# Batch 0 of a fused linear attention and SwiGLU kernel: both halves of q loaded in fp32 by one queue, q turned by products onto a bank of ones, order redone

## The chip, the cores and the metric

The kernel runs on one core of one Trainium2 chip. The metric is the device time of one execution in microseconds. Seven executions of the kernel before took 314.73 us in the median (314.56 to 316.13).

A core has five engines with an instruction stream each: TensorE (PE, products into PSUM; PEld is its loading of weights), VectorE (DVE), ScalarE (ACT, which computes exp, ln and silu), GpSimd (POOL) and SyncE (SP). In this kernel POOL and SP issue the transfers: POOL those that also convert fp32 to fp16 on the way, SP those that do not convert. Each engine works through its own stream in program order and waits on semaphores.

## The reference

Inputs q, k, v have the shape (8 batches, 8 heads, 576 positions, 64). With phi(x) = x + 1 for x > 0 and exp(x) otherwise:

```
kv  = einsum('bhsd,bhse->bhde', phi(k), v)
z   = sum over s of phi(k)
num = einsum('bhsd,bhde->bhse', phi(q), kv)
den = einsum('bhsd,bhd->bhs', phi(q), z) + 1e-06
x   = (num / den), heads side by side: 4608 tokens x 512
out = ((silu(x @ w_gate) * (x @ w_val)) @ w_out)      # 512 -> 1536 -> 512
```

The feed-forward part has nearly all of the products: 4608 x 512 x 1536 twice and 4608 x 1536 x 512 once.

## The kernel before

**Tiling.** Nine groups (g = 0 to 8) of 512 tokens each go through the feed-forward part. A group takes eight units of 64 tokens; a batch has nine units (J = 9), so group 0 is made of the first eight units of batch 0. The main loop (L626) runs over groups: twelve blocks of 128 columns of w_gate and w_val (`l1`, L287; products L291), each followed by silu and multiplication (`l1_post`, L280), then four output tiles (`l2_mm`, L297; products L298). The attention of later batches is slipped in between.

**The head.** Group 0 can only start when batch 0's attention has given x^T. Lines 331 to 481 do that in an order written out by hand (`manual_schedule`); each engine follows the order of the lines. The eight heads are worked on as two halves of four, called lp 0 and lp 1: lp picks the half in every transfer and tile.

The steps of batch 0, with the names used later:

- Transfers. SP loads q's lp 0 into `q32` and k's lp 0 into `k32`, both in fp32 (L332). POOL loads q's lp 1 (L334), k's lp 1, v, and the weights, all to fp16 (L102, L111).
- `warm(n, w)` (L121) issues n products of ones that nothing reads; `WARM` holds their counts. They keep TensorE active.
- q: the fp32 half is cast to fp16 `qr` by VectorE (L431) and ScalarE (L432). `qtr` (L365) transposes q on TensorE into fp16 PSUM. phi is then applied to the transposed q, three steps for 1024 columns (`t_phi`, L380): exp by ScalarE into `qT`, min(exp, 1) by VectorE (L382), and max(q, 0) added by VectorE (L383). For lp 1 the last step is split into two halves of 512 (`t_add_half`, L420).
- k: exp by ScalarE (`ek`, L436 and `exp_k`), max(k, 0) by VectorE (`kp`, L437 and `mx_k`), min(exp, 1) by VectorE (`mn_k`, L144). The two parts are never added: products take `kp` and then `ek` into the same accumulator.
- z: `zt` (L392) sums the positions by products with a matrix of ones; `zr_copy` (L397) copies the sum to `Zr`.
- kv: `kv_corner` (L178, products L184) takes 72 small products per lp; `r_copy` (L194) copies them to `R`.
- den and num: `t_corners` (L416, products L253) multiplies qT by Zr or R. `lnrd` (L401) makes 1/den by ScalarE as exp(-ln(den)), two ln and two exp steps per lp.
- x: `x_t` (L412) multiplies num by 1/den on VectorE (L410) into xT, four tiles of 128 x 512 over lp and half.
- The first two blocks of group 0 are run by `l1_mm` (L272, products L275) chunk by chunk of xT, so that they can start before all of xT is there.

The PSUM pairs are named `pp4`; X and Y are pairs made of halves of two of them. The order of the lines also fixes what stands in each engine's stream behind a wait.

Of the kernel before, what the change touches and what calls it, by code (L numbers as in the profile page):

```python
# [7 lines left out]
FP32 = mybir.dt.float32  # L8
FP16 = mybir.dt.float16
# [4 lines left out]
P = 128  # L14
# [3 lines left out]
def kernel(  # L18
# [21 lines left out]
    EPS = 1e-6  # L40
    SC = 4096.0
    NB = 3
    WARM = (32, 8, 8, 6, 3, 3)

    sb = ctx.enter_context(tc.tile_pool(name="sb", bufs=1))
    pp = ctx.enter_context(tc.tile_pool(name="ps", bufs=1, space=bass.MemoryType.PSUM))
# [15 lines left out]
    Zr = many([P, 2, 2, D], FP16, "Zr")  # L62
    rd = many([P, 2, 512], FP16, "rd")

    q32 = sb.tile([P, 2, J * D], FP32, name="q32")
# [19 lines left out]
    idx = sb.tile([P, P], mybir.dt.int32, name="idx")  # L85
    gate = sb.tile([P, 1], FP16, name="gate")
    epsb = sb.tile([P, 1], FP32, name="epsb")

    pp4 = [[pp.tile([P, 512], FP32, name=f"pp_{2 * i + e}") for e in range(2)] for i in range(4)]
    ring = list(pp4)  # L90
# [27 lines left out]
    def act(out, in_, func=AF.Copy, scale=1.0, bias=0.0):  # L118
        nc.scalar.activation(out=out, in_=in_, func=func, bias=bias, scale=scale)  # L119
# [9 lines left out]
    def jl(t, b, lp):  # L129
        return t[b % 2][:, lp, :, :].rearrange("p j (l d) -> p l j d", d=D)  # L130
# [4 lines left out]
    def exp_k(b, lp):  # L135
        act(jl(ek, b, lp), lj(kr, b, lp), AF.Exp)
# [248 lines left out]
    def t_phi_main(b, lp, ps):  # L385
        return t_phi(qT[b][:, lp, 0:8, :, :].rearrange("p j h c -> p (j h c)"), ps[:, :].bitcast(FP16))
# [30 lines left out]
        for (b, j0, j1, c0) in units(g)[1]:  # L417
            corners(ps, W[b], b, lp, j0, j1, c0)

    def t_add_half(lp, ps, h):  # L420
        a = qT[0][:, lp, 4 * h:4 * h + 4, :, :].rearrange("p j h c -> p (j h c)")
        nc.vector.scalar_tensor_tensor(out=a, in0=ps[:, 256 * h:256 * h + 256].bitcast(FP16), scalar=0.0, in1=a,  # L422
                                       op0=ALU.max, op1=ALU.add)

    k32v = k32[:, :, :].rearrange("p l (j d) -> p l j d", d=D)
    pq = pp4[0]
    kvp[0] = pp4[1]
    X = [pp4[0][0], pp4[3][0]]
    Y = [pp4[3][1], pp4[0][1]]
    ph = [t_phi_main(0, lp, pq[lp]) for lp in range(2)]  # L430
    nc.vector.tensor_copy(out=qr[0][:, 0, :], in_=q32[:, 0, :])  # L431
# [5 lines left out]
    nc.vector.tensor_scalar(out=jl(kp, 0, 0), in0=k32v, scalar1=0.0, scalar2=None, op0=ALU.max)  # L437
    warm(WARM[1])
    zt(0, 0, X[1], kp, True, False)
    ph[0][1]()  # L440
    ph[0][2]()
    warm(WARM[2], 2)
    qtr(0, 1, pq[1])
    ph[1][0]()
    exp_k(0, 1)
    mn_k(0, 0)
    warm(WARM[3], 2)
    zt(0, 0, X[1], ek, False, True)
    zr_copy(0, 0, X[1])
    mx_k(0, 1)  # L450
    warm(WARM[4], 2)
    t_corners(0, Zr, 0, pp4[2])
    lnrd(pp4[2], 0)
    ph[1][1]()
    zt(0, 1, Y[0], kp, True, False)
    t_add_half(1, pq[1], 0)
# [5 lines left out]
    t_add_half(1, pq[1], 1)  # L462
    zr_copy(0, 1, Y[0])
    t_corners(0, R, 0, X)
    t_corners(0, Zr, 1, Y)
    lnrd(Y, 1)
    x_t(0, 0, X, (0,))
    kv_corner(0, 1, kp, True, False)
    kv_corner(0, 1, ek, False, True)
    x_t(0, 0, X, (1,))  # L470
    r_copy(0, 1, 2, "VV")
    l1_mm(0, 0, pp4[2], (0,))
    l1_mm(0, 1, X, (0,))
    t_corners(0, R, 1, pp4[1])
    x_t(0, 1, pp4[1])
    for c in (1, 2, 3):
        l1_mm(0, 0, pp4[2], (c,))
# [259 lines left out]
```

## Time and profile before

| | |
|---|---|
| median of seven executions | 314.73 us (314.56 to 316.13) |
| profiled execution, its time | 316.34 us |
| profiled execution, its span | 314.6 us |
| TensorE busy | 307.1 us (98% of the span) |
| VectorE busy | 204.0 us (65%) |
| ScalarE busy | 151.4 us (48%) |
| mean granted TensorE clock | 0.995 |
| first product of the main loop (L291) | 20.14 us after the start of the span |

The span runs from the first to the last instruction; the execution's time has 1.74 us around it. The profile gives, for a stretch of the span, each engine's busy time, the granted clock of TensorE (1.00 is full) and what the transfers moved. The timeline lists instructions in order of time; in square brackets stands how long the engine had been idle before, and which event ended that. "issue" there means that the engine waited for nothing that the profile shows.

### The profile page before, as it was taken

The page shows a single profiled execution, that of the slowest core. Times are in us where ns is not written, and L with a number is a line of the kernel's source. Part 1 is how long each engine was busy: PE and PEld are TensorE (multiplying, and loading weights), DVE is VectorE, ACT ScalarE, POOL GpSimd, SP SyncE. Part 2 cuts the span into 40 slices and gives each one's busy share as a digit, 9 for nine tenths or more (in the row PEclk, how much of TensorE's full clock was granted, in tenths as well). Part 3 has the DMA queues.
Part 4 walks back from the last instruction along what each step waited for, and adds up shares of the span by engine and source line. Part 5 has one row for each costly group of instructions (what it writes and reads, how often), then busy time and mean ns, then how long its engine had stood idle before and what let it go on. Part 6 is the DMA issues. An engine that isn't in the chain of part 4 may idle for free.

```text
span 314.6 us, 5728 instructions
## 1 busy us (share of the span) xinstructions
PE 307.1 (98%) x2289; PEld 145.8 (46%) x2289; DVE 204.0 (65%) x357; ACT 151.4 (48%) x229; POOL 47.4 (15%) x72
## 2 busy tenths in 40 slices
PE   7899999999999999999999999999999999999994
PEld 6534444444544454445444544444444444444442
DVE  3744788899789666978598749874991434134420
ACT  5844839738653755356435743475331333133311
POOL 8655345300000230023000500000000000000000
PEclk9989999999999999999999999999999999999999
DMA  8999999994612396129703890314022400140014
GB/s 217 199 198 200 206 207 226 244 206 83 140 33 39 52 181 168 37 40 162 200 11 65 119 243 1 75 33 102 2 56 60 94 2 1 33 102 0 0 35 100
DMA packets 41163, 32.82 MB, mean 104 GB/s; under 512 B 16432, under 2 KB 36144, under 8 KB 41136
## 3 DMA queue, kind: packets, MB, share of 16 engines
q0 software_dynamic: 20464, 18.29, 37.0%
q1 hardware_dynamic: 20592, 14.13, 18.5%
q8 instruction: 18, 0.29, 0.3%
q14 instruction: 9, 0.07, 0.1%
q10 hardware_dynamic: 80, 0.03, 0.0%
HBM read 37.75 MB, written 9.44 MB: 150 GB/s over the span
## 4 chain that ended last, share of the span: by engine, by line
PE 95%; DMA 1%; DVE 1%; issue 0%; SPq 0%; ACT 0%
PE pp L291 57%; PE pp L298 30%; PE pp L275 3%; PE pp L253 2%; PE pp L184 2%; DMA k<-in_k_dram 1%; PE pp L123 1%; PE pp L369 1%; DVE qT L422 0%; DVE kp L437 0%; PE pp L211 0%; PE pp L394 0%; DVE osb L321 0%; DVE Zr L398 0%; SPq L332 0%
## 5 line engine op out<-in xcount | busy, mean ns | idle before, releaser
L119 ACT ACTIVATE sil<-pp 128x512 f16<-128x512 f32 x108 | 63.4, 597 | 103.5 <-PE pp L291 97.4
L291 PE MATMUL pp<-xT,wg 128*128 128x512 f16 x416 | 106.8, 379 | 0.0
L291 PE MATMUL pp<-xT,wv 128*128 128x512 f16 x416 | 106.8, 379 | 0.0
L284 DVE SCALAR_TENSOR_TENSOR hT<-pp,sil 128x512 f16<-128x512 f32 x108 | 72.3, 681 | 49.4 <-PE pp L291 35.7
L298 PE MATMUL pp<-wo,hT 128*128 128x512 f16 (+2 forms) x444 | 97.2, 374 | 0.6 <-DVE osb L321 0.6
L298 PEld LDWEIGHTS <-hT 128*128 128x128 f16 x444 | 41.8, 98 | 49.8 <-issue 2.1
L291 PEld LDWEIGHTS <-wv 128*128 128x128 f16 x416 | 40.7, 98 | 49.1
L291 PEld LDWEIGHTS <-wg 128*128 128x128 f16 x416 | 40.7, 98 | 48.4
L321 DVE TENSOR_SCALAR osb<-pp 128x512 f32<-128x512 f32 (+1 forms) x19 | 12.9, 682 | 30.7 <-PE pp L298 30.7
L119 ACT ACTIVATE osb<-pp 128x512 f32<-128x512 f32 (+1 forms) x18 | 10.3, 574 | 34.8 <-PE pp L298 34.8
L119 ACT ACT_TABLE_LOAD x13 | 16.7, 1283 | 2.3 <-PE pp L291 2.1
L119 ACT ACTIVATE ek<-kr 128x1152 f16<-128x1152 f16 x15 | 16.8, 1155 | 0.1
L228 DVE TENSOR_TENSOR qp<-qp,rden 128x1152 f16<-128x1152 f16 x12 | 16.2, 1347 | 0.0
L219 DVE TENSOR_REDUCE den<-prod 128x18 f32<-128x1152 f16 x12 | 16.1, 1344 | 0.0
L668 POOL COPY gate<-qT 128x1 f16<-128x1 f16 x4 | 1.0, 256 | 99.3 <-DMA qT<-qp 99.3
L119 ACT ACTIVATE eq<-qr 128x1152 f16<-128x1152 f16 x12 | 13.2, 1147 | 0.0
L270 DVE TENSOR_SCALAR xT<-pp 128x512 f16<-128x512 f32 (+1 forms) x14 | 8.8, 667 | 6.6 <-PE pp L253 6.6
L102 POOL DMA_DIRECT2D vr<-in_v_dram x16 | 11.6, 728 | 9.2 <-PE pp L291 3.4
L102 POOL DMA_DIRECT2D qr<-in_q_dram x15 | 10.9, 732 | 7.8 <-DMA vr<-in_v_dram 1.9
L102 POOL DMA_DIRECT2D kr<-in_k_dram x15 | 10.8, 720 | 7.5 <-DMA wo<-in_moe_w_out_dram 1.9
L146 DVE TENSOR_SCALAR ek<-ek 128x1152 f16<-128x1152 f16 x16 | 7.7, 479 | 6.5 <-ACT ek L119 6.5
L158 DVE TENSOR_TENSOR kp<-ek,kp 128x1152 f16<-128x1152 f16 x14 | 10.6, 758 | 0.5
(71 smaller groups left out, 186.6 us busy)
## 6 DMA issues: line engine op xcount, KB each, us to landing
out_dram<-osb SPq DMA_DIRECT2D x70, 128.0 KB, 3.3
vr<-in_v_dram POOLq DMA_DIRECT2D x16, 288.0 KB, 10.0
qr<-in_q_dram POOLq DMA_DIRECT2D x15, 288.0 KB, 11.4
kr<-in_k_dram POOLq DMA_DIRECT2D x15, 288.0 KB, 9.6
wo<-in_moe_w_out_dram POOLq DMA_DIRECT2D x3, 512.0 KB, 13.0
wg<-in_moe_w_gate_dram POOLq DMA_DIRECT2D x5, 256.0 KB, 9.5
wv<-in_moe_w_val_dram POOLq DMA_DIRECT2D x5, 256.0 KB, 9.0
q<-in_q_dram SPq DMA_DIRECT2D x1, 576.0 KB, 3.7
```

Of the source, the lines that this page charges most:

```text
L102: nc.gpsimd.dma_start(out=dst[b % NB][:, 2 * lp:2 * lp + 2, :], in_=src[b].rearrange("(l a) (c j) d -> (a c) l (j d)", a=2, j=J)[:, 2 * lp ...
L119: nc.scalar.activation(out=out, in_=in_, func=func, bias=bias, scale=scale)
L146: nc.vector.tensor_scalar(out=a, in0=a, scalar1=1.0, scalar2=None, op0=ALU.min)
L158: nc.vector.tensor_tensor(out=a, in0=ek[b % 2][:, lp, :, :], in1=a, op=ALU.add)
L219: nc.vector.tensor_reduce(out=den[:, c, :], in_=prod[:, :, :].rearrange("p j (l d) -> p (j l) d", d=D), axis=AX.X, op=ALU.add)
L228: nc.vector.tensor_tensor(out=qv, in0=qv, in1=rden[:, c, :].unsqueeze(2).to_broadcast([P, 2 * J, D]), op=ALU.mult)
L270: nc.vector.tensor_scalar(out=dst, in0=ps[l2][:, c0:], scalar1=1.0 / SC, scalar2=None, op0=ALU.mult)
L275: nc.tensor.matmul(out=ps[h][:, :], lhsT=w[:, c, P * fb:P * fb + P], rhs=xT[g % 2][:, c, :], start=(c == 0), stop=(c == 3))
L284: nc.vector.scalar_tensor_tensor(out=hT[g % 2][:, fb, :], in0=ps[1][:, :], scalar=SC, in1=s[:, :], op0=ALU.mult, op1=ALU.mult)
L291: nc.tensor.matmul(out=ps[h][:, :], lhsT=w[:, c, P * fb:P * fb + P], rhs=xT[g % 2][:, c, :], start=(c == 0), stop=(c == 3))
L298: nc.tensor.matmul(out=l2p[(g, t)][:, n0:n1], lhsT=hT[g % 2][:, fb, P * t:P * t + P], rhs=wo[:, fb, n0:n1], start=(fb == 0), stop=(fb == F ...
L321: nc.vector.tensor_scalar(out=o[:, n0:n1], in0=ps[:, n0:n1], scalar1=1.0 / SC, scalar2=None, op0=ALU.mult)
```

## The change

It touches batch 0's head alone.

- SP now loads q's lp 0, q's lp 1 and k's lp 0, in this order, all in fp32 (`q32` is twice as large). POOL's load of q's lp 1 goes.
- The lp 1 half of q is cast to fp16 by two casts on VectorE.
- q is no longer transposed into fp16 PSUM. `q_one` first fills two PSUM pairs with ones, by products of a matrix of 1/128 with ones (each 512 columns wide); `q_turn` adds the transposed q to that by products with the identity. PSUM then holds q + 1 in fp32.
- phi is exp(PSUM - 1), by ScalarE (`q_exp`), and min(max(PSUM, 1), exp), by VectorE (`q_phi`): one VectorE step in the place of two, in pieces of 512 columns.
- The numbers and widths of the fillers change, and one run of them is added ahead of the first feed-forward products.
- The order changes: both halves of q are turned and given exp before k's exp; the second half's q_phi comes after both k halves' steps; Zr's corners of lp 1 come before R's of lp 0; the second R's corners come between the first two products of `l1_mm` and the rest.

```diff
-    WARM = (32, 8, 8, 6, 3, 3)
+    WARM = (20, 14, 30, 4, 3, 3)
...
-    def warm(n, w=1, ps=None):
+    def warm(n, w=128, ps=None):
         for _ in range(n):
-            nc.tensor.matmul(out=(ps or pp4[2][1])[:, 256:256 + P * w], lhsT=ones[:, :],
-                             rhs=ones[:, :].unsqueeze(1).to_broadcast([P, w, P]), start=True, stop=True)
+            nc.tensor.matmul(out=(ps or pp4[1][1])[:, 256:256 + w], lhsT=ones[:, :],
+                             rhs=ones[:, 0:1].to_broadcast([P, w]), start=True, stop=True)
...
-    for (src, dst) in ((q, q32), (k, k32)):
-        nc.sync.dma_start(out=dst[:, :, :],
-                          in_=src[0].rearrange("(l a) (c j) d -> (a c) l (j d)", a=2, j=J)[:, 0:2, :])
-    ld(q, qr, 0, 1)
+    for (src, dst, h) in ((q, q32, 0), (q, q32, 2), (k, k32, 0)):
+        nc.sync.dma_start(out=dst[:, h:h + 2, :],
+                          in_=src[0].rearrange("(l a) (c j) d -> (a c) l (j d)", a=2, j=J)[:, h:h + 2, :])
...
+    nc.vector.memset(part[:, :], 1.0 / P)
...
+    nc.vector.memset(m1[:, :], -1.0)
...
+    def q_one(pair_):
+        for h in range(2):
+            nc.tensor.matmul(out=pair_[h][:, :], lhsT=part[:, :], rhs=ones[:, 0:1].to_broadcast([P, 512]),
+                             start=True, stop=False)
+
+    def q_turn(lp, pair_):
+        for l2 in range(2):
+            for j in range(J - 1):
+                nc.tensor.matmul(out=pair_[j // 4][D * l2:D * l2 + D, P * (j % 4):P * (j % 4) + P],
+                                 lhsT=qr[0][:, 2 * lp + l2, D * j:D * j + D], rhs=id16[:, :],
+                                 start=False, stop=(j % 4 == 3))
+
+    def q_half(lp, h):
+        return qT[0][:, lp, 4 * h:4 * h + 4, :, :].rearrange("p j h c -> p (j h c)")
+
+    def q_exp(lp, h, pair_):
+        act(q_half(lp, h), pair_[h][:, :], AF.Exp, bias=m1[:, 0:1])
+
+    def q_phi(lp, h, pair_):
+        a = q_half(lp, h)
+        nc.vector.scalar_tensor_tensor(out=a, in0=pair_[h][:, :], scalar=1.0, in1=a, op0=ALU.max, op1=ALU.min)
...
+    qa, qb = pp4[2], pp4[0]
     nc.vector.tensor_copy(out=qr[0][:, 0, :], in_=q32[:, 0, :])
     act(qr[0][:, 1, :], q32[:, 1, :])
+    nc.vector.tensor_copy(out=qr[0][:, 2, :], in_=q32[:, 2, :])
+    nc.vector.tensor_copy(out=qr[0][:, 3, :], in_=q32[:, 3, :])
     warm(WARM[0])
-    qtr(0, 0, pq[0])
-    ph[0][0]()
+    q_one(qa)
+    q_one(qb)
+    q_turn(0, qa)
+    q_exp(0, 0, qa)
+    q_exp(0, 1, qa)
+    warm(WARM[1], 64)
+    q_turn(1, qb)
+    q_exp(1, 0, qb)
+    q_exp(1, 1, qb)
+    warm(WARM[2], 64)
     act(jl(ek, 0, 0), k32v, AF.Exp)
+    exp_k(0, 1)
+    q_phi(0, 0, qa)
+    q_phi(0, 1, qa)
     nc.vector.tensor_scalar(out=jl(kp, 0, 0), in0=k32v, scalar1=0.0, scalar2=None, op0=ALU.max)
...
+    mn_k(0, 0)
     zt(0, 0, X[1], kp, True, False)
...
+    warm(WARM[3], 256)
     zt(0, 0, X[1], ek, False, True)
     zr_copy(0, 0, X[1])
...
+    warm(WARM[4], 256)
     t_corners(0, Zr, 0, pp4[2])
     lnrd(pp4[2], 0)
...
+    mx_k(0, 1)
     mn_k(0, 1)
+    q_phi(1, 0, qb)
+    q_phi(1, 1, qb)
     kv_corner(0, 0, kp, True, False)
     kv_corner(0, 0, ek, False, True)
+    zt(0, 1, Y[0], kp, True, False)
     zt(0, 1, Y[0], ek, False, True)
+    zr_copy(0, 1, Y[0])
     r_copy(0, 0, 1, "VV")
...
     t_corners(0, Zr, 1, Y)
     lnrd(Y, 1)
-    x_t(0, 0, X, (0,))
+    t_corners(0, R, 0, X)
+    x_t(0, 0, X)
     kv_corner(0, 1, kp, True, False)
     kv_corner(0, 1, ek, False, True)
-    x_t(0, 0, X, (1,))
     r_copy(0, 1, 2, "VV")
+    warm(WARM[5], 256, pp4[2][1])
     l1_mm(0, 0, pp4[2], (0,))
+    t_corners(0, R, 1, pp4[1])
     l1_mm(0, 1, X, (0,))
-    t_corners(0, R, 1, pp4[1])
     x_t(0, 1, pp4[1])
```

More of the change, by code (lines that the diff above doesn't have):

```diff
@@ L63 @@
     rd = many([P, 2, 512], FP16, "rd")
-    q32 = sb.tile([P, 2, J * D], FP32, name="q32")
+    q32 = sb.tile([P, HL, J * D], FP32, name="q32")
     k32 = sb.tile([P, 2, J * D], FP32, name="k32")
@@ L87 @@
     epsb = sb.tile([P, 1], FP32, name="epsb")
+    m1 = sb.tile([P, 1], FP32, name="m1")
+    part = sb.tile([P, P], FP16, name="part")
     pp4 = [[pp.tile([P, 512], FP32, name=f"pp_{2 * i + e}") for e in range(2)] for i in range(4)]
@@ L418, in t_corners @@
             corners(ps, W[b], b, lp, j0, j1, c0)
[L420 to L423, printed above, removed]
+    def q_one(pair_):
[15 more added lines that the diff above has]
+        nc.vector.scalar_tensor_tensor(out=a, in0=pair_[h][:, :], scalar=1.0, in1=a, op0=ALU.max, op1=ALU.min)
     k32v = k32[:, :, :].rearrange("p l (j d) -> p l j d", d=D)
-    pq = pp4[0]
     kvp[0] = pp4[1]
@@ L429 @@
     Y = [pp4[3][1], pp4[0][1]]
-    ph = [t_phi_main(0, lp, pq[lp]) for lp in range(2)]
+    qa, qb = pp4[2], pp4[0]
     nc.vector.tensor_copy(out=qr[0][:, 0, :], in_=q32[:, 0, :])
     act(qr[0][:, 1, :], q32[:, 1, :])
+    nc.vector.tensor_copy(out=qr[0][:, 2, :], in_=q32[:, 2, :])
+    nc.vector.tensor_copy(out=qr[0][:, 3, :], in_=q32[:, 3, :])
     warm(WARM[0])
-    qtr(0, 0, pq[0])
-    ph[0][0]()
+    q_one(qa)
[8 more added lines that the diff above has]
+    warm(WARM[2], 64)
     act(jl(ek, 0, 0), k32v, AF.Exp)
+    exp_k(0, 1)
+    q_phi(0, 0, qa)
+    q_phi(0, 1, qa)
     nc.vector.tensor_scalar(out=jl(kp, 0, 0), in0=k32v, scalar1=0.0, scalar2=None, op0=ALU.max)
-    warm(WARM[1])
+    mn_k(0, 0)
     zt(0, 0, X[1], kp, True, False)
[L440 to L447, printed above, removed]
+    warm(WARM[3], 256)
     zt(0, 0, X[1], ek, False, True)
     zr_copy(0, 0, X[1])
-    mx_k(0, 1)
-    warm(WARM[4], 2)
+    warm(WARM[4], 256)
     t_corners(0, Zr, 0, pp4[2])
     lnrd(pp4[2], 0)
-    ph[1][1]()
-    zt(0, 1, Y[0], kp, True, False)
-    t_add_half(1, pq[1], 0)
+    mx_k(0, 1)
     mn_k(0, 1)
+    q_phi(1, 0, qb)
+    q_phi(1, 1, qb)
     kv_corner(0, 0, kp, True, False)
     kv_corner(0, 0, ek, False, True)
+    zt(0, 1, Y[0], kp, True, False)
     zt(0, 1, Y[0], ek, False, True)
+    zr_copy(0, 1, Y[0])
     r_copy(0, 0, 1, "VV")
-    t_add_half(1, pq[1], 1)
-    zr_copy(0, 1, Y[0])
-    t_corners(0, R, 0, X)
     t_corners(0, Zr, 1, Y)
     lnrd(Y, 1)
-    x_t(0, 0, X, (0,))
+    t_corners(0, R, 0, X)
+    x_t(0, 0, X)
     kv_corner(0, 1, kp, True, False)
     kv_corner(0, 1, ek, False, True)
-    x_t(0, 0, X, (1,))
     r_copy(0, 1, 2, "VV")
+    warm(WARM[5], 256, pp4[2][1])
     l1_mm(0, 0, pp4[2], (0,))
+    t_corners(0, R, 1, pp4[1])
     l1_mm(0, 1, X, (0,))
-    t_corners(0, R, 1, pp4[1])
     x_t(0, 1, pp4[1])
```

## The prediction

> **What bounds the kernel now.** I read the page first (share of the span, slices, chain), then the first 21 us by windows of 1 us, then the timeline of that stretch. Times below are us from the start of the span.
>
> ```profile
> span 314.6 us, 5728 instructions
> ...
> PE   7899999999999999999999999999999999999994
> ...
> PE 95%; DMA 1%; DVE 1%; issue 0%; SPq 0%; ACT 0%
> ```
>
> TensorE carries the chain from about 20 us to the end, and nothing there is edited. So the change is worth exactly what it moves one event: the first product of L291, at 20.14. Ahead of it TensorE waits for others, and once its clock falls. Windows of 1 us (columns: busy time of PE, PEld, DVE, ACT, POOL, then the granted clock, DMA share, GB/s):
>
> ```profile
> 14.00:15.00 1.00, 0.86 (x59) 0.79 (x59) 0.00 (x0) 1.00 (x2) 0.60 (x1) 0.69 1.47 200
> 15.00:16.00 1.00, 1.00 (x4) 0.37 (x4) 0.36 (x2) 0.95 (x3) 1.00 (x3) 0.50 1.44 194
> 16.00:17.00 1.00, 1.00 (x6) 0.13 (x4) 0.00 (x0) 1.00 (x1) 0.72 (x2) 0.50 1.44 194
> 17.00:18.00 1.00, 1.00 (x7) 0.28 (x4) 0.50 (x1) 0.13 (x1) 0.63 (x1) 0.60 1.51 212
> 18.00:19.00 1.00, 1.00 (x6) 0.47 (x5) 0.79 (x2) 0.00 (x0) 0.74 (x1) 1.00 1.38 187
> ```
>
> The clock is halved from 14.38 to 17.80 (the shares 0.69 and 0.60 give the edges). The 3.41 us before that were thin:
>
> ```profile
> 10.97:14.38 3.41, 1.94 (x114) 1.29 (x104) 2.97 (x8) 3.25 (x6) 1.67 (x3) 1.00 1.43 193
> ```
>
> The timeline of the same stretch, cut to the events that the change moves (start, duration, engine, line):
>
> ```profile
> 4.48 0.46 DVE L431 CAST qr<-q 128x576 f16<-128x576 f32 x1 [1.15 <-DMA q<-in_q_dram]
> 5.91 0.76 DVE L437 TENSOR_SCALAR kp<-k 128x1152 f16<-128x1152 f32 x1 [0.98 <-DMA k<-in_k_dram]
> 6.80 1.15 ACT L119 ACTIVATE ek<-k 128x1152 f16<-128x1152 f32 x1
> 7.48 1.23 DVE L383 SCALAR_TENSOR_TENSOR qT<-pp,qT 128x1024 f16<-128x1024 f16 x1
> 8.62 0.45 DVE L146 TENSOR_SCALAR ek<-ek 128x1152 f16<-128x1152 f16 x1
> 9.60 0.29 DVE L398 TENSOR_SCALAR Zr<-pp 128x128 f16<-128x128 f32 x1 [0.52 <-PE pp L394]
> 10.60 0.68 ACT L119 ACTIVATE lnt<-pp,epsb 128x512 f32<-128x512 f32 x1
> 10.62 0.69 DVE L422 SCALAR_TENSOR_TENSOR qT<-pp,qT 128x512 f16<-128x512 f16 x1
> 14.14 0.38 PE L184 MATMUL pp<-vr,kp 64*64 64x64 f16 x22 [0.81 <-issue]
> 16.75 0.64 PE L253 MATMUL pp<-qT,R 64*64 64x512 f16 x4
> 17.50 1.29 DVE L410 SCALAR_TENSOR_TENSOR xT<-pp,rd 128x512 f16<-128x512 f32 x2 [2.13 <-PE pp L253]
> 20.14 1.03 PE L291 MATMUL pp<-xT,wg 128*128 128x512 f16 x4
> ```
>
> The reader is to see that VectorE (L437 to L410) is nearly unbroken from 5.9 to 13.9 while k's exp is done at 7.96 and waits for L383; and that at 14.14 TensorE stops for 0.81 in the middle of one group (after 14 of 36 products with the same inputs), put down to "issue". The instruction queue moved one block of 16 KB between 11.8 and 12.9, so I read the stop as a wait for instructions.
>
> **What the low clock cost.** At full clock L275 products follow each other by 0.216 (18.63, 18.85), at half by 0.42. Redone at full clock from 14.14: rest of the kv products to 14.62, four L275 to 15.49, corners of R at 15.49, x from 16.0 to 17.3, eight more products behind a 0.15 wait, L291 at 18.5. The drop cost 20.14 - 18.5 = 1.64. The profiled execution took 316.34; without the drop 314.70, which is the median shown (314.73, lowest 314.56). So I take the median execution as one with little or no drop, and the executions above 315 as ones that met it. The fair rival of the new head is 18.5.
>
> **The change, part by part.**
>
> SP's queue: one transfer more there, one fewer on POOL. q's first half lands as before (4.48), the second takes k's place (5.91), k is third. SP's issue (0.45) delays nobody: SP's next work is the output. POOL's first 0.83 issue goes, so idx and the masks come earlier, hidden, since id16 is first needed at 4.99. First k landed 1.43 after q, so third it lands at 7.34 if SP's data go ahead of POOL's, and at 8.77 if POOL's take every second packet. From 2 to 5 us, with POOL's transfers issued from 1.25 on, only SP's queue moved data:
>
> ```profile
> q1 hardware_dynamic: 469, 1.04, 95.9%
> ```
>
> I take 7.34. The Trainium skill (DMA: Bandwidth & Descriptors, Issuing engines are not separate DMA queues) says that transfers of all issuing engines interleave on the same 16 DMA engines and that another issuer saves only issue time; this speaks against the move and for 8.77, and the row above disagrees for this stretch. By the rule the sum below ends 0.1 later. POOL's data start 1.4 later with 1.4 less of q in them, so k's other half (8.9), v and the weights keep their times.
>
> First products: 20 fillers at 0.107 (32 took 3.41) and four 512-wide ones onto the ones bank (0.43 at half, 0.22 at full clock) end by 4.9 at the latest; q's cast, needed first, is ready at 4.94. Nothing. Two memsets (0.17, 0.06): hidden by the same wait.
>
> VectorE: out go two L382 (0.43), L383 (1.23), two L422 (0.69), 3.47; in come four steps like L422 and L410 (0.69, next start 0.61 later) and two casts (0.46, next start 0.38 later), 3.68. ScalarE: out two exps of 1024 (1.02), in four of 512 like lnt (0.68, next start 0.58 later): +0.4. So no engine is relieved; what counts is order.
>
> In order: q's first products as L369 (4.99), exps from 5.8 and 6.4. Casts of the second half 5.91 and 6.29, to 6.75. Fillers of 64 columns have no row; between 0.03 (half of L123's 0.056) and 0.056 each, I take the upper, since the same weights are loaded; 14 end by 6.6, 30 by 9.0, beside the waits. Second products end 7.4, exps 7.4 and 8.0, so ScalarE is free at 8.55. Only then k's exp: 8.55 to 9.7, against 7.96 before. VectorE: the two steps of q's first half 6.66 and 7.27, max of k 7.88 to 8.64, then it stands for k's exp, with max and min of the other k half and the second q steps queued behind. L146 at 9.75 (+1.13), Zr at 10.7, corners 11.05, ln/exp from 11.6 instead of 10.60; their eight steps (10.60 to 15.83 before) end at 16.8. VectorE from 10.7: 0.21, 0.37, 0.37 (Zr, max, min), two of 0.61, Zr 0.20, R 0.35: R at 13.4, against 11.95.
>
> Corners of R on TensorE at 13.45. Here the products before them number 223, the number before the stop at 14.14 of the old kernel, so the instruction wait should fall here. Bounds: nothing, or until 14.14 as before (+0.6). The block before it ends in the second filler run, at about 7.6, against about 8.0 in the old order, so I take 13.55, nearer the lower. Then x at 14.1 and 14.7 to 15.3, R copies to 15.65, corners of the second R at 15.7 (15.49 in the old kernel at full clock), and 14 instead of 12 products behind them: 14 x 0.216 + 0.22 = 3.24. x is ready in time (16.9, 17.6 for products at 17.2, 18.1). L291 at 18.95.
>
> **Sum.** 18.95 against 20.14: -1.19 on the profiled execution, 316.34 - 1.19 = 315.15; against the 314.73 of the median, +0.4. No drop of the clock is in it. By start-to-start spacing (36 kv products 0.30, a zt run 0.2, four corners 0.22, a wide filler 0.11) the window that lost the clock held about 1.1 us of products: 0.14 and 0.34 of kv, 0.2, two times 0.22. The thinnest 3.41 us of the new order, 10.2 to 13.6, holds 2.0: kv 0.6, zt 0.6, three fillers 0.33, corners 0.44. Nothing shows where between 1.1 and 2.0 the limit lies. The Trainium skill (TensorE: Matmul & The Clock Gate, What's actually happening) halves the clock after an idle window of about 3.4 us; the trace lost it after a window that was half busy. By the rule neither kernel would lose the clock and the sum would be the same 18.95 against 18.5.
>
> 0.3% (0.94 us) is about what a measurement of this kernel can tell from no change.
>
> **Rivals.**
> (a) Slower: the clock falls in the new kernel too. Between about 10 and 15.7 TensorE waits for Zr, R and x; if a window of that stretch counts as thin, the 3.41 us after it do half of their work: +1.7 where all of them are products, about +0.8 where half falls on waits, 315.95 to 316.85. It decides if more than half of the executions meet it. For it: the waits go on until 15.7, in the old kernel to 14.6. Against: the fillers and all kv products lie inside them.
> (b) Slower: the instruction block comes as late as before, at 14.14: corners of R wait 0.6 more, 315.75.
> (c) Faster: k's exp is not late, because the half-size exps overlap more than I charge (0.50 between the two sil), and the steadier clock also takes away the 0.17 to 1.6 that half of the executions now lose: 18.2, 314.4. It passes the bound where L291 starts 1.4 earlier than forecast, at 17.55 (313.75).
> (d) No effect: the head ends where it did, 314.7.
>
> **Chances.** Forecast (314.8 to 315.6, its own range) 0.47; (a) 0.18, of which 0.15 over the bound; (b) and other lateness past 315.7 0.12; (c) 0.15, of which 0.11 under 313.8; (d) 0.08. Slower 0.27, faster 0.11, same 0.62. The range leaves out the faster tail of (c) and the full price of (a): 314.2 to 316.4.
>
> **What would show it.** Right: q's second cast pair at 5.9; exp of k at 8.5 with VectorE idle before L146 until about 9.7; Zr near 10.7; R near 13.4; corners of the second R near 15.7 as the last wait of TensorE; clock 1.00 from 5 us on; L291 near 19.0. Wrong: a clock of 0.5 after 11 us, an "issue" stop beyond 13.6, k landing after 8.5, or L291 before 18.3.

## The result and the profile after

The changed kernel takes 318.47 us in the median of twelve executions, against 315.29 for the kernel before in 31 executions. The ratio is 1.0091, with a 95% interval of 1.0066 to 1.0116, so the change is slower by 0.9%. The forecast was 315.15 with a range of 314.2 to 316.4, and it is missed on the slow side, by 3.3 us.

The profile that came with the changed kernel is of an execution that no other resembles: 1822.38 us, all of it on TensorE, whose products of 512 columns took 1.7 us each while the profile gave a granted clock of 1.00. From its page:

```profile
span 1820.6 us, 5776 instructions
...
L293 PE MATMUL pp<-xT,wg 128*128 128x512 f16 x416 | 589.3, 1707 | 0.0
```

It tells nothing of the change, whose other eleven executions took 316.89 to 320.27. I therefore ran the changed kernel again, unedited, and read the result from that profile (318.80 us, clock 0.987; median of five 318.80, ratio 1.011, 1.0071 to 1.0149). It is the first of the experiments.

> The changed kernel itself, unedited, once more, since its first profile shows a TensorE at about a sixth of its rate throughout (512-wide products 1.7 us apart) and can't be laid beside the old one. Three theories for the 2.9 us that it lost. Clock: the granted clock is 0.5 in one or two stretches of 3.4 us before 21 us, and the first product of the main loop (L293) starts at 21 to 23, each stretch in product work costing up to 1.7. Instructions: an idle of TensorE put down to issue, over 0.8 us long, ahead of L293, at a clock of 1.00. Late k: the max of k (L469) starts after 9 because k lands late, and all that follows with it. If none shows and L293 starts near 19, the loss is in the main loop, and the shares of L293 and L300 there have grown.

The lines of its page that answer to those shown of the kernel before:

```profile
span 317.0 us, 5776 instructions
...
PE   8699999999999999999999999999999999999994
...
PE 91%; DVE 3%; DMA 3%; ACT 1%; SPq 0%; issue 0%; DVEq 0%
PE pp L293 56%; PE pp L300 27%; DMA k<-in_k_dram 3%; PE pp L277 2%; PE pp L255 2%; PE pp L186 2%; DVE qT L386 1%; ACT ek L121 1%; PE pp L125 0%; ACT L582 0%; DVE qT L385 0%; DVE ek L148 0%; PE pp L397 0%; SPq L334 0%; DVE kp L160 0%
```

The second digit of PE's slices is 6 where it was 8. The chain that ended last has 3% of the span on one transfer of k, which had 1% before. The chain of the first 26 us, in order of time (start, duration, what), says the same more sharply:

```profile
1.76 8.02 DMA k<-in_k_dram
9.78 0.02 issue
9.80 1.17 ACT ek L121
10.98 0.02 issue
11.00 0.72 DVE ek L148
```

From SP's third issue at 1.76 until 9.78 the kernel's end depends on nothing but k's way into the chip. The timeline has the events that the prediction named:

```profile
5.83 0.46 DVE L452 CAST qr<-q 128x576 f16<-128x576 f32 x1 [1.12 <-DMA q<-in_q_dram]
7.28 1.27 ACT L121 ACTIVATE qT<-pp,m 128x512 f16<-128x512 f32 x2 [0.29 <-PE pp L431]
9.80 1.16 ACT L121 ACTIVATE ek<-k 128x1152 f16<-128x1152 f32 x1 [1.26 <-DMA k<-in_k_dram]
10.62 0.39 PE L397 MATMUL pp<-ob,kp 128*128 128x2 f16 x9 [2.12 <-DVE kp L469]
12.20 0.29 DVE L401 TENSOR_SCALAR Zr<-pp 128x128 f16<-128x128 f32 x1 [0.49 <-PE pp L397]
18.82 0.41 PE L255 MATMUL pp<-qT,R 64*64 64x512 f16 x4
22.19 1.03 PE L293 MATMUL pp<-xT,wg 128*128 128x512 f16 x4
```

The reader is to see three things. The second half of q is cast at 5.83 and ScalarE is through with q's exps at 8.55, as forecast. Then ScalarE stands for 1.26, until k is there. And TensorE, its run of 30 fillers done, stands for 2.12 ahead of the first products of k. In windows (busy time of PE, PEld, DVE, ACT, POOL, then the granted clock, DMA share, GB/s):

```profile
9.00:10.00 1.00, 0.00 (x0) 0.00 (x0) 0.20 (x1) 0.20 (x1) 0.48 (x1) 1.00 1.21 214
...
11.00:12.00 1.00, 0.71 (x14) 0.41 (x12) 0.71 (x1) 1.00 (x1) 0.45 (x1) 0.94 1.35 195
12.00:13.00 1.00, 1.00 (x13) 0.46 (x14) 0.80 (x3) 0.02 (x1) 0.00 (x0) 0.50 1.46 191
...
18.00:19.00 1.00, 1.00 (x7) 0.15 (x5) 0.04 (x1) 0.98 (x2) 0.56 (x1) 0.65 1.39 187
8.47:11.88 3.41, 0.99 (x18) 0.66 (x18) 1.47 (x2) 2.15 (x3) 1.49 (x2) 1.00 1.24 213
```

TensorE was busy for 0.99 of the 3.41 us before 11.88, and from there the clock is 0.50 for 6.8 us, two such stretches. By the shares 0.94 and 0.65 the half clock lasts from 11.88 to 18.7.

The first product of the main loop starts at 22.19, 3.24 later than the 18.95 forecast. That part of the frame held: in every profile of this study but that of 1822 us the execution's time is this start plus 296.2 to 296.6 us (before: 316.34 - 20.14 = 296.20; here 318.80 - 22.19 = 296.61). So the 3.24 are nearly all of the 3.65 by which this execution missed the forecast; the other 0.41 lie behind L293, and no run explains them. The question is what the 3.24 are made of.

### The profile page after: what moved, and what is told of

Read it like the earlier page. It is cut to its first block, busy times and chain, and to the rows that moved or that the text cites. A ratio compares the mean times of both kernels' runs of the same rounds, so it can differ in the third digit from the quotient of the medians.

```text
span 1820.6 us, 5776 instructions
## 1 busy us (share of the span) xinstructions
PE 1815.1 (100%) x2310; PEld 484.9 (27%) x2310; DVE 211.2 (12%) x360; ACT 156.2 (9%) x231; POOL 46.5 (3%) x71
## 4 chain that ended last, share of the span: by engine, by line
PE 100%; DVE 0%; issue 0%; ACT 0%
PE pp L293 60%; PE pp L300 31%; PE pp L277 2%; PE pp L255 2%; PE pp L186 1%; PE pp L125 1%; PE pp L431 0%; PE pp L372 0%; PE pp L425 0%; PE pp L213 0%; PE pp L397 0%; PE pp L380 0%; DVE osb L323 0%; DVE Zr L401 0%; ACT osb L121 0%
## 5 line engine op out<-in xcount | busy, mean ns | idle before, releaser
L293 PE MATMUL pp<-xT,wg 128*128 128x512 f16 x416 | 589.3, 1707 | 0.0
L293 PE MATMUL pp<-xT,wv 128*128 128x512 f16 x416 | 589.0, 1706 | 0.0
L300 PE MATMUL pp<-wo,hT 128*128 128x512 f16 (+2 forms) x444 | 574.5, 1658 | 0.6 <-DVE osb L323 0.6
L300 PEld LDWEIGHTS <-hT 128*128 128x128 f16 x444 | 136.1, 310 | 410.6 <-issue 409.3
L293 PEld LDWEIGHTS <-wv 128*128 128x128 f16 x416 | 134.3, 323 | 415.6 <-issue 415.6
L293 PEld LDWEIGHTS <-wg 128*128 128x128 f16 x416 | 135.1, 325 | 410.9 <-issue 410.9
L186 PEld LDWEIGHTS <-kp 64*64 64x64 f16 x576 | 27.2, 351 | 11.8 <-issue 11.6
L277 PE MATMUL pp<-xT,wv 128*128 128x512 f16 x16 | 27.5, 1720 | 0.0
L277 PE MATMUL pp<-xT,wg 128*128 128x512 f16 x16 | 26.6, 1663 | 0.0
L186 PE MATMUL pp<-vr,kp 64*64 64x64 f16 x576 | 26.6, 450 | 0.0
L255 PE MATMUL pp<-qT,R 64*64 64x512 f16 (+7 forms) x128 | 25.7, 1023 | 0.0
L125 PE MATMUL pp<-ones 128*128 128x64 f16 (+2 forms) x74 | 20.8, 580 | 1.1 <-DVE ones L356 1.1
L121 ACT ACT_TABLE_LOAD x13 | 16.7, 1283 | 20.0 <-PE pp L293 19.8
```

The lines of the kernel that those rows point to most:

```text
L125: nc.tensor.matmul(out=(ps or pp4[1][1])[:, 256:256 + w], lhsT=ones[:, :], rhs=ones[:, 0:1].to_broadcast([P, w]), start=True, stop=True)
L186: nc.tensor.matmul(out=ps[hh][D * l2:D * l2 + D, D * lp:D * lp + D], lhsT=t[b % 2][rows, lp, j, D * l2:D * l2 + D], rhs=vr[b % NB][rows, 2 ...
L255: nc.tensor.matmul(out=ps[l2][C * hh:C * hh + C, c0:c0 + C * (j1 - j0)], lhsT=W[rows, lp, hh, :], rhs=qt(b, lp, hh, j0, j1)[rows], start=T ...
L277: nc.tensor.matmul(out=ps[h][:, :], lhsT=w[:, c, P * fb:P * fb + P], rhs=xT[g % 2][:, c, :], start=(c == 0), stop=(c == 3))
L293: nc.tensor.matmul(out=ps[h][:, :], lhsT=w[:, c, P * fb:P * fb + P], rhs=xT[g % 2][:, c, :], start=(c == 0), stop=(c == 3))
L300: nc.tensor.matmul(out=l2p[(g, t)][:, n0:n1], lhsT=hT[g % 2][:, fb, P * t:P * t + P], rhs=wo[:, fb, n0:n1], start=(fb == 0), stop=(fb == F ...
```

## The experiments

The theory after the result: k's third place on SP's queue costs far more than I priced, because POOL's transfers run beside it; the idle TensorE then loses its clock. Rivals: the clock alone (k late, but hidden if the clock held), the new order with k's exp behind all of q's, the new arithmetic, and TensorE's instruction stream, which the change of the fillers shifts.

### Where k's transfer goes: POOL's data

The DMA queues of the changed kernel from 5.2 to 9.2 us (packets, MB, share of 16 engines), q1 being SP's queue and q0 POOL's:

```profile
q0 software_dynamic: 418, 0.46, 69.0%
q1 hardware_dynamic: 276, 0.60, 43.4%
```

And those of the kernel before in the same stretch:

```profile
q0 software_dynamic: 729, 0.80, 117.9%
q1 hardware_dynamic: 32, 0.04, 2.7%
```

In the kernel before, SP is as good as done when POOL's data begin, and only 0.04 MB are left to it. In the changed kernel SP still has one whole transfer, and gets 0.60 MB in 4.0 us, 150 GB/s, against the 348 GB/s it had from 2 to 5 us in the kernel before; of the packets POOL's queue has 418, SP's 276. MB are those written; POOL's fp16 has twice that to read. The start of POOL's data hardly moves: 5.18 in the kernel before, 4.89 here, each after a first issue on POOL at 1.25 and 1.35. In these two kernels the start thus follows POOL's issue by 3.5 to 3.9 us, whether SP has a whole transfer left or only 0.04 MB.

The first test: the changed kernel with POOL's first transfer issued at 2.42 instead of 1.35. A tiny copy on ScalarE waits for its table load, and POOL waits for that copy; the memsets move ahead with it.

```diff
+    act(tick[:, :], ones[:, 0:1])
+    nc.gpsimd.tensor_copy(out=gate[:, :], in_=tick[:, :])
```

> The changed kernel with POOL's first transfer held back by about 1.2 us (a copy that waits for a step of ScalarE at 2.2). Theory sharing: POOL's data begin near 6.2 instead of 4.9, k's transfer is nearly done by then and lands at 7.3 to 7.8 instead of 9.8; its exp starts at 8.6, the first product of the main loop is at 19.0 to 19.5, about 315.5 us, a little later where v or the weights come 1.2 later. Rival (a third transfer on SP's own queue is slow by itself): k still lands after 9, and with POOL's loads late too the time is 318 or more.

Measured: median 315.70 of ten (315.16 to 318.54) against 314.90, ratio 1.0029 (0.9993 to 1.0065). Of the 3.3 us by which the forecast was missed, 2.8 are back in the median. The fastest execution, 315.16, comes to the forecast 315.15, but the fastest of ten is not what the forecast was for. In the profiled execution (316.51 us) POOL's data begin at 6.49, and SP's queue is alone from 5.2 to 6.4, moving 317 GB/s:

```profile
q1 hardware_dynamic: 175, 0.38, 96.6%
```

k still lands at 9.31 there, and not at the 7.3 to 7.8 expected: 0.20 MB of it are left at 6.4, and the last 0.06 MB take from 7.0 to 9.0 beside POOL's.

```profile
9.31 1.17 ACT L122 ACTIVATE ek<-k 128x1152 f16<-128x1152 f32 x1 [0.45 <-DMA k<-in_k_dram]
20.17 1.03 PE L294 MATMUL pp<-xT,wg 128*128 128x512 f16 x4
```

So the tail of a transfer that the other queue catches is stretched too, and this execution is 0.8 slower than the median.

The second test goes further: ScalarE first fills a scratch tile with ones, so that POOL's first transfer is issued at 3.61.

```diff
+    act(prod[:, :, :], ones[:, :].unsqueeze(1).to_broadcast([P, J, P]))
+    act(tick[:, :], prod[:, 0, 0:1])
+    nc.gpsimd.tensor_copy(out=gate[:, :], in_=tick[:, :])
```

> The changed kernel with POOL's first transfer held back further (ScalarE first writes 1152 columns that nothing uses, 1.15 us): it is issued near 3.5, its data begin near 7.1, after the last of k's. Theory sharing: k lands at 7.2 to 7.5 instead of 9.8 and the recorded chain applies: k's exp 8.5, Zr 10.7, R 13.4, corners of the second R 15.7, first product of the main loop 18.9 to 19.3, 315.2 to 315.6 us. If k's landing were not the first cause, or the order and the new arithmetic cost more than the recorded +0.4, it stays at 19.8 or later, 316.2 or more.

Measured: median 316.29 of twelve (315.38 to 318.44), ratio 1.0034 (1.0013 to 1.0055). It is no better than the first test, and by the words of the expectation (L294 at 19.8 or later, 316.2 or more) it went to the rival. POOL's data begin at 6.56, hardly later, although the first transfer was issued 1.19 later; what else sets their start isn't shown. The clock fell here too: five of the twelve executions have a mean clock of 0.993 or lower, as three of the ten of the first test have. The seven of each that kept it (0.997 or higher) have a median of 315.62 in both tests, 0.5 above the forecast. The profiled execution (316.75) kept the clock, but had the second half of q at 6.95 instead of 5.83. This gives a look at the forecast chain with a late start and a full clock. Timeline:

```profile
6.95 0.63 DVE L457 CAST qr<-q 128x576 f16<-128x576 f32 x1 [2.24 <-DMA q<-in_q_dram]
...
9.60 1.16 ACT L122 ACTIVATE ek<-k 128x1152 f16<-128x1152 f32 x1
11.74 0.29 DVE L406 TENSOR_SCALAR Zr<-pp 128x128 f16<-128x128 f32 x1 [0.48 <-PE pp L402]
16.91 0.54 PE L256 MATMUL pp<-qT,R 64*64 64x512 f16 x4
20.41 1.03 PE L294 MATMUL pp<-xT,wg 128*128 128x512 f16 x4
```

Against the forecast (8.55, 10.7, 15.7, 18.95) these are 1.05, 1.04, 1.21 and 1.46 later. Behind k's exp the forecast was therefore light by 0.4 in this profile, and by 0.5 in that of the first test (20.17 - 9.31 = 10.86 against 10.40).

The third test puts the new transfers alone into the kernel before (its casts of q's second half with them, everything else old):

```diff
-    for (src, dst) in ((q, q32), (k, k32)):
+    for (src, dst, h) in ((q, q32, 0), (q, q32, 2), (k, k32, 0)):
...
-    ld(q, qr, 0, 1)
+    nc.vector.tensor_copy(out=qr[0][:, 2, :], in_=q32[:, 2, :])
+    nc.vector.tensor_copy(out=qr[0][:, 3, :], in_=q32[:, 3, :])
```

> The old kernel with the new transfers alone: SP loads both halves of q and then k in fp32, POOL one load fewer, VectorE casts the second half of q; order, arithmetic and fillers as they were. Theory sharing: k lands at 9.7, its exp follows, TensorE idles ahead of the sums over k and the clock falls: first product of the main loop at 21 to 23, 317 to 319.5 us, so the transfers alone give all of the loss or more. Theory order: within 1 us of the old kernel.

Measured: median 320.42 of four (319.97 to 320.62) against 314.90, ratio 1.0149 (1.0089 to 1.0209), more than the 317 to 319.5 expected. k lands at 10.37:

```profile
10.37 1.17 ACT L119 ACTIVATE ek<-k 128x1152 f16<-128x1152 f32 x1 [3.65 <-DMA k<-in_k_dram]
11.19 0.40 PE L393 MATMUL pp<-ob,kp 128*128 128x2 f16 x9 [4.98 <-DVE kp L438]
```

TensorE stands for 5.0 us ahead of it, and the clock is 0.50 from 8.48 to 15.3. The transfers alone cost 5.5 us in the old order, so where k is late, the new order, arithmetic and fillers together are worth 1.6 to 2.0 us (318.80 and 318.47 against 320.42). Together the rows of the queues and the three runs show the cause: k's transfer gets less of the DMA engines as soon as POOL's data flow, and the transfers alone are enough to lose the time. No profile shows the chain with k at 7.34: with POOL held back the end of k's transfer was still caught (its last packet ended at 8.98 in the first test, at 8.07 in the second).

### The clock

Eighteen fillers of 256 columns go into the wait for k:

```diff
     warm(WARM[2], 64)
+    warm(18, 256)
```

> The changed kernel with 18 more fillers of 256 columns (2.0 us at full clock) ahead of the first sum over k, where TensorE stood idle for 2.1 us. Theory clock (late k costs 1.1 to 1.6 us by itself, and the idle that it makes costs the clock, another 2): the clock stays at 1.00, the first product of the main loop moves from 22.2 to 20.1 to 20.4, about 316.5 us. Rival (the clock falls for the thin stretch after 11 us whatever fills the wait): still a clock of 0.5 over one or two stretches of 3.4 us, 317.5 to 319.

Measured: median 317.19 of ten (316.89 to 318.12), ratio 1.0053 (1.0025 to 1.0081). The window that was nearly empty is filled, and the clock holds through to the end:

```profile
12.00:13.00 1.00, 0.73 (x12) 0.45 (x12) 0.51 (x3) 0.48 (x1) 0.00 (x0) 1.00 1.44 191
...
8.47:11.88 3.41, 2.80 (x31) 2.05 (x29) 1.18 (x2) 1.66 (x3) 1.41 (x2) 1.00 1.23 220
```

k landed later than in the run above (10.26 against 9.78), and L293 still started earlier (20.93 against 22.19). From k's exp to L293 it took 20.93 - 10.26 = 10.67, against 22.19 - 9.80 = 12.39 with the low clock; the drop cost 1.72. This splits the 3.24: 9.80 - 8.55 = 1.25 for k's landing, 1.72 for the clock, and the rest, 0.27, for steps behind k's exp that were priced light (10.67 against 18.95 - 8.55 = 10.40).

### The order, with the old transfers

The changed kernel with the transfers of the kernel before (k second on SP's queue, q's second half by POOL), to see what order and arithmetic do by themselves:

```diff
-    for (src, dst, h) in ((q, q32, 0), (q, q32, 2), (k, k32, 0)):
+    for (src, dst) in ((q, q32), (k, k32)):
...
+    ld(q, qr, 0, 1)
...
-    nc.vector.tensor_copy(out=qr[0][:, 2, :], in_=q32[:, 2, :])
-    nc.vector.tensor_copy(out=qr[0][:, 3, :], in_=q32[:, 3, :])
```

> The changed kernel with the transfers of the old one: SP loads q's first half and k, POOL loads q's second half to fp16 ahead of the rest, the two casts go. Theory sharing (k is late because from 5 us on POOL's transfers share the DMA engines with SP's third one): k lands at 5.9 as in the old kernel, q's second half at 7.3; in the new order ScalarE still gives q's second half its exps first, so k's exp starts near 9.3 and the first product of the main loop is at 19.6 where the clock holds, about 315.8 us. Theory order (the new order and the fillers lose the time, whatever the transfers do): it stays within 1 us of the changed kernel, 317.5 to 319.

Measured: median 316.76 of ten (315.92 to 317.67), ratio 1.0048 (1.0019 to 1.0077), between the 315.8 of the one theory and the 317.5 of the other. k is in time, but its exp is not:

```profile
8.00 1.27 ACT L121 ACTIVATE qT<-pp,m 128x512 f16<-128x512 f32 x2 [0.59 <-PE pp L432]
...
9.16 1.16 ACT L121 ACTIVATE ek<-k 128x1152 f16<-128x1152 f32 x1
```

ScalarE waits for q's second half and does k's exp behind it, at 9.16, where the kernel before had it at 6.80. So the new order needs q's second half early, which is what the new transfers give; they give it at k's cost. In the profiled execution (317.39) the clock also fell, from 13.89 to 17.30; three others show a mean clock as low (0.992 to 0.996). The six that kept it took 315.92 to 317.06, so with the old transfers the new order, arithmetic and fillers lose 1 us or more against the 314.90 of the kernel before, whatever the clock does.

### The arithmetic alone, and the instruction stream

The kernel before with the new arithmetic of q in the old order, with the old transfers. Its first fillers are 20, and with the four products of ones there are eight products fewer ahead of the rest than in the kernel before.

```diff
-    warm(WARM[0])
-    qtr(0, 0, pq[0])
-    ph[0][0]()
+    warm(20)
+    q_one(qa)
+    q_one(qb)
+    q_turn(0, qa)
+    q_exp(0, 0, qa)
+    q_exp(0, 1, qa)
...
-    ph[0][1]()
-    ph[0][2]()
+    q_phi(0, 0, qa)
+    q_phi(0, 1, qa)
```

> The old kernel with the new arithmetic alone: old transfers, old order, old fillers but for the first run (20 and the four wide products onto the ones); q is turned onto the bank of ones, phi in halves of 512 columns with one step of VectorE each. By the rows VectorE is freed of 0.45 us for each half, but the stop of TensorE for instructions at 14.1 and the weights' landing at 14.4 stay where they are: within 0.5 us of the old kernel, 314.5 to 315.2. If the new arithmetic is slow by itself (four half-size exps, products into fp32 PSUM), 316 or more.

Measured: median 316.25 of twelve (315.40 to 318.36), ratio 1.0043 (1.0019 to 1.0067). Six of the twelve have a mean clock of 0.995 or lower; the other six took 315.40 to 315.64. By the words of the expectation a median over 316 speaks for an arithmetic that is slow by itself. But the timeline has a stop "issue" in the same group of 36 products as the kernel before, but after 22 products and not after 14:

```profile
13.37 0.35 PE L186 MATMUL pp<-vr,kp 64*64 64x64 f16 x22
14.88 0.31 PE L186 MATMUL pp<-vr,kp 64*64 64x64 f16 x14 [1.16 <-issue]
```

Eight products fewer ahead, eight products later: the stop sits at a fixed place of TensorE's stream, after 223 products in both kernels. To tell the arithmetic from the stream, I gave the same kernel 36 first fillers of 64 columns, 40 products with those of ones:

```diff
-    warm(20)
+    for _ in range(36):
+        nc.tensor.matmul(out=pp4[1][1][:, 256:320], lhsT=ones[:, :], rhs=ones[:, 0:64], start=True, stop=True)
```

> The old kernel with the new arithmetic alone, as before, but the first run of fillers is 36 of 64 columns in the place of 20 of 128 (about the same time, 16 more products in TensorE's stream). Theory instructions (TensorE's stop in the kv products comes at a fixed place of its stream, and the block of instructions that it waits for is asked for a fixed number of products earlier): the stop moves from after 22 of the 36 products to after 6 of them, and ends earlier, at 14.2 or before in the place of 14.88; the first product of the main loop comes 0.5 to 0.9 earlier than 19.36, 314.6 to 315.0 us in the undisturbed executions in the place of 315.4 to 315.6. Rival (the new arithmetic is slow by itself): the stop ends as late as before, 315.4 or more.

Measured: median 314.31 of thirteen (314.22 to 318.17) against 314.95, ratio 0.9974 (0.9959 to 0.9989). The profiled execution was the slowest one, 318.17, in which k landed at 8.68, so its trace says little of the median. I ran the kernel once more, unedited, to see the number repeat.

> The old kernel with the new arithmetic and 36 first fillers once more, unedited, for a second measurement and for a profile in which k lands in time (in the first profile it landed at 8.7). Theory instructions: the stop in the kv products comes after 6 of 36 and ends at 14.2 or before, or is gone; first product of the main loop at 18.0 to 18.4; 0.2 to 0.3% below the old kernel again. Rival (the first measurement was luck of the clock): within 0.1% of the old kernel.

Measured: median 314.30 of thirteen (314.07 to 315.77) against 314.88, ratio 0.9974 (0.9957 to 0.9991). The number repeats, but the profile is again of the slowest execution (315.77): k landed at 7.34 and L293 started at 19.51, not at 18.0 to 18.4. The 36 products have no stop over 0.3 us there.

The control is the kernel before with nothing but its first fillers changed, so that the stream is as much shorter as in the first of these kernels:

```diff
-    warm(WARM[0])
+    warm(8, 2)
+    warm(16)
```

> The old kernel, its first 32 fillers of 128 columns replaced by 8 of 256 and 16 of 128: the same time on TensorE, 8 products fewer in its stream, nothing else. Theory instructions: the stop moves from after 14 to after 22 of the 36 kv products and ends 0.3 to 0.8 later, at 14.5 to 14.9; 0.3 to 0.9 us slower than the old kernel in the undisturbed executions. Rival (the stop is a wait for data): place and time unchanged, 314.5 to 314.7.

Measured: median 317.59 of six (315.91 to 317.96) against 314.95, ratio 1.0069 (1.0044 to 1.0093). Twenty-four products take the time of 32, and the kernel loses 2.6 us. The stop is after 22 products here too, and longer; it ends at 15.68, where 14.5 to 14.9 was expected:

```profile
13.38 0.35 PE L184 MATMUL pp<-vr,kp 64*64 64x64 f16 x22
15.68 0.31 PE L184 MATMUL pp<-vr,kp 64*64 64x64 f16 x14 [1.95 <-issue]
```

The clock then fell too, from 16.56 to 19.98. Five of the six executions have a mean clock of 0.995 or lower; the sixth kept it and took 315.91, so by that one execution the longer stop costs 1.0 and the clock the rest.

And the other way, eight products more, of the kernel before's 32 fillers 24 kept and 16 of half the width added:

```diff
-    warm(WARM[0])
+    warm(24)
+    for _ in range(16):
+        nc.tensor.matmul(out=pp4[2][1][:, 256:320], lhsT=ones[:, :], rhs=ones[:, 0:64], start=True, stop=True)
```

> The old kernel, its first 32 fillers of 128 columns replaced by 24 of 128 and 16 of 64: the same number of columns, 8 products more in TensorE's stream, nothing else. Theory instructions: the stop in the kv products moves from after 14 to after 6 of the 36 and ends 0.2 to 0.7 earlier than 14.14; the median falls to 314.2 to 314.5, as low as with the new arithmetic and 36 first fillers (314.3), and the gain there is the fillers' alone. Rival (the new arithmetic is what gains there): within 0.1 us of the old kernel, 314.6 to 314.9.

Measured: median 314.37 of twelve (314.08 to 314.94) against 314.92, ratio 0.9978 (0.9964 to 0.9993). The stop is gone:

```profile
13.38 0.51 PE L184 MATMUL pp<-vr,kp 64*64 64x64 f16 x36
...
18.07 1.03 PE L291 MATMUL pp<-xT,wg 128*128 128x512 f16 x4
```

The clock was 1.00 from 5.6 us on, and none of the twelve executions took over 315 us, where six of the seventeen of the kernel before beside them did. So the 0.2% that the arithmetic with 36 fillers wins over the kernel before is won by the fillers alone; the arithmetic adds nothing that I can measure, in either direction.

The place of the stop and its end are two things. The place is the same in every profile that has such a stop: after 223 products of TensorE, also in the kernel with both cures below, and with the old transfers, where it is short (0.30, at 14.66). The end is in the instruction queue (q8). The one block of 16 KB that it moves in this stretch starts, by the trace's packets, at 10.77 with eight products more, at 11.87 in the kernel before, at 12.64 with the arithmetic alone and at 13.26 with eight fewer. The three stops ended at 14.14, 14.88 and 15.68, in each case 2.2 to 2.4 us after that. In none of the thirteen profiles (that of 1822 us left out) does product 224 start earlier than 2.24 us after the packet. With eight more it was due at 13.42, 2.65 us after it, and did not have to wait. What sets when the block is moved isn't shown: 197 products had started before it in the kernel before and with the arithmetic alone, 201 with eight fewer and 123 with eight more, so the "fixed number of products earlier" of the expectation is not borne out. The Trainium skill (Runtime: NRT & Kernel Launch, Instruction fetch mechanics) says that an engine's stream is fetched in blocks of 16 KB or 256 instructions and that the cost of crossing a boundary is mostly hidden. The trace has such blocks (packets of 0.02 MB), but here the cost is not hidden: 0.81, 1.16 and 1.95 us.

### Putting the two cures together

POOL's first transfer later, and half as many fillers in the wait for k:

```diff
+    act(tick[:, :], ones[:, 0:1])
+    nc.gpsimd.tensor_copy(out=gate[:, :], in_=tick[:, :])
...
+    warm(9, 256)
```

> The changed kernel with both causes lessened: POOL's first transfer held back by 1.2 us as before, and 9 more fillers of 256 columns (1.0 us) where TensorE waited for k. If late k and the clock that falls behind it are the whole difference to the recorded chain, the clock stays at 1.00 in nearly all executions and the median comes to 315.2 to 315.8, against 318.5 of the changed kernel and the recorded 315.15. If a third cause is at work it stays above 316.2.

Measured: median 316.85 of twelve (316.11 to 317.80) against 314.88, ratio 1.0035 (1.0007 to 1.0062). This missed: it is slower than POOL later alone. In its profile the clock holds, but the nine added products shift the stream, and the stop, again after 223 products, now falls on the chain to the second Zr:

```profile
13.06 0.24 PE L401 MATMUL pp<-ob,ek 128*128 128x2 f16 x4
14.13 0.27 PE L401 MATMUL pp<-ob,ek 128*128 128x2 f16 x5 [0.82 <-issue]
```

A cure that adds instructions to TensorE's stream thus has a price of its own. The best kernels of the study are the old transfers and order with eight more products among the first fillers, with the old arithmetic (314.37) or the new (314.30).

## Why the prediction was wrong, point by point

**The frame: right.** The change is worth what it moves the first product of the main loop. With the start known, each profile's time follows within 0.4 us.

**"I take 7.34", k's landing: wrong, and the step that failed.** It landed at 9.78, and at 10.26 and 10.37 in two other profiles with these transfers. Both ends of the bound were too early. I read the row of 2 to 5 us, in which only SP's queue moved data, as SP's data going ahead of POOL's. It only showed that POOL's had not yet begun. The next stretch of the same trace would have told: POOL's data begin 3.9 us after its first issue, at 5.18, and k, not done until 5.91, does not keep them back. The consequence drawn in the same paragraph, that POOL's data start 1.4 later, failed for that reason too. The upper bound let POOL take every second packet, which is half of SP's rate; SP's queue fell to 150 GB/s from 348, to less than half, with 276 of 694 packets.

The rule of the Trainium skill that I had set against my row (DMA: Bandwidth & Descriptors, Issuing engines are not separate DMA queues) was right on the direction: the transfers of both queues do interleave, the moment both have data. What the runs add is that they do not interleave before, as POOL's begin late.

**The price of that: 0.1 by the rule, 1.25 measured.** The 0.1 was itself light: 8.77 is 0.22 behind the 8.55 of the sum. I let k be late at little cost because its exp was to wait for q's until 8.55 anyway. That cover was right (ScalarE was through at 8.55 in the profile), but it ended 1.2 us before k came.

**q's halves, the casts, the exps: right.** 4.25 and 5.83 against 4.48 and 5.91; the last exp of q ended at 8.55 as worked out.

**"No drop of the clock is in it": wrong, as a consequence.** I weighed the stretch from 10.2 to 13.6, where I expected TensorE to be half busy. With k late, the thin window was an earlier one, 8.47 to 11.88, with 0.99 busy. Rival (a) named the mechanism and its size (0.8 to 1.7; measured 1.72), but placed it behind Zr, on the waits for Zr, R and x, and gave it 0.18. How large the risk is with k at 7.34 no run shows; with POOL held back 8 of 22 executions have a mean clock of 0.993 or lower. With k late it was the rule: 13 of the 16 executions of the changed kernel other than that of 1822 us show one. One more term of mine lies in that window: I took the fillers of 64 columns at 0.056 each, and they started 0.031 apart, so that the run of 30 ended at 8.49 and not at 9.0. I had not joined the two: lateness of a transfer and loss of the clock are not independent cases, since the first makes the idle window of the second. The Trainium skill's rule of an idle window of about 3.4 us (TensorE: Matmul & The Clock Gate, What's actually happening) would not have warned: TensorE was busy for 29% of the window.

**The chain behind k's exp: right within 0.3 to 0.5.** From exp of k to L293 forecast 10.40, measured 10.67 with a full clock, 10.81 with POOL last, 10.86 with POOL later.

**Rival (b), the instruction block: did not happen in the changed kernel.** There was no stop "issue" over 0.3 us beyond 13.6. The chain itself was late: the block's packet starts at 11.06 in its profile, and product 224 only at 15.74. That it was worth naming is shown by the other kernels, where it cost up to 1.95 us.

**Rivals (c) and (d): did not happen.** With POOL held back the fastest executions, 315.16 and 315.38, come to the forecast sum. They have no profile, so it isn't shown that k was in time in them. The fastest of the kernel before beside them took 314.47 and 314.55, so even there the change loses 0.7 to 0.8 us, where the forecast had 0.4 against the median.

**Left open.** Why single packets of q or k come late in some executions (q's second half at 6.95, k at 8.68 with the old transfers) isn't shown. Nor is what separates windows that lose the clock from those that keep it (below). Removing POOL's transfers from the stretch altogether wasn't tried, since k's other half and v are needed soon after.

## What to carry to other kernels

A queue that has moved no data yet is not a queue with lower priority: look up when its first data come after its first issue, and price every transfer that is still unfinished then at the shared rate. A late transfer also empties TensorE, so the clock's price belongs to the same case, not to another one. And fillers are instructions: whoever changes their number moves the block boundaries of the stream, which should be looked for as "issue" stops in the middle of a group; here narrower fillers in larger number gained 0.2% at no work.

## What the runs showed of the hardware beyond expectation

- POOL's first data came 3.0 to 4.1 us after its first issue in five profiles (1.25 to 5.18, 1.35 to 4.89, 1.34 to 4.87, 2.42 to 6.49, 3.61 to 6.56), with a whole transfer of SP's unfinished or only its last packets.
- With both queues running, SP's moved 150 GB/s and POOL's wrote 115 GB/s (0.46 MB in 4.0 us); SP's alone 317 to 348.
- The busy time of a window does not decide alone whether the clock falls. Within a profile the records of the clock begin a whole number of 3.41 us apart. Of the windows of this grid ahead of the main loop, the five at full clock with 0.99, 1.15, 1.16, 1.47 and 1.94 us of TensorE's work lost it, and those with 2.03 or more kept it, but for one with 2.47 (10.48 to 13.89, the run with the old transfers). What sets that one apart stays open.
- Ahead of the first record of the clock, which comes 3.7 to 7.1 us into the span, the page gives 1.00, but products run slower: the first sixteen turns of q took 0.89 us where the record came at 5.05 (changed kernel) and 1.50 us where it came at 7.06 (the run with the old transfers).
- A boundary of the instruction stream can stop TensorE for 0.81 to 1.95 us, and eight products more or fewer ahead of it decide whether it does and for how long; it came after 223 products each time.
- One execution of the changed kernel ran its products at a sixth of the pace from beginning to end, with a granted clock of 1.00 in the profile. It did not come again in the 70 further executions of it and of the kernels made from it, nor in those of the kernel before.
